# Sorted block attention with Fourier mixing on one core: the second half of V mixed in its own layout and turned through device memory

## The chip, the cores and the metric

The kernel runs on one core of a Trainium2 chip. The core has five engines with a queue of instructions each: TensorE (PE, with its weight loads PEld), VectorE (DVE), ScalarE (ACT), GpSimd (POOL) and SyncE (SP), the last two used here mostly to issue transfers. Data lies in on-chip memory with 128 partitions; PE writes its sums into eight PSUM banks of 128 partitions by 512 numbers, which DVE or ACT must empty. The metric is the time of one launch in microseconds on the device, smaller is better. The kernel before takes 257.36 us (median of three runs, 257.14 to 257.45).

## The reference

There are 4 batches, 8 heads, 768 positions and 64 channels per head, and the positions form 8 blocks of 96. A small 8×8 matrix per head, normalised five times over rows and columns, mixes the blocks of K and V; each block of Q attends to the one block at its place.

```python
for _ in range(5):
    P = P - np.max(P, axis=-1, keepdims=True)
    P = np.exp(P)
    P = P / (np.sum(P, axis=-1, keepdims=True) + 1e-09)
    P = P / (np.sum(P, axis=-2, keepdims=True) + 1e-09)
k_sorted = np.einsum('bhij,bhjcd->bhicd', P, k_b).reshape(B, H, S, D)
v_sorted = np.einsum('bhij,bhjcd->bhicd', P, v_b).reshape(B, H, S, D)
scores = scale * np.matmul(q_b, k_sb.transpose(0, 1, 2, 4, 3))
attn = softmax(scores);  x = heads_joined(np.matmul(attn, v_sb))
```

The heads are joined to x of 4 × 768 × 512, and the second part mixes it by a Fourier transform and sends it through a LayerNorm and a feed-forward network (FFN) of width 2048:

```python
u = x + np.real(np.fft.fft(np.fft.fft(x, axis=1), axis=2))
un = (u - mu) / np.sqrt(var + 1e-06)          # mean, variance over 512
out = u + np.maximum(un @ w_ch1, 0.0) @ w_ch2
```

## The kernel before

The matrices are normalised first, for all 32 pairs of batch and head. Then the four batches follow each other; the attention of later batches runs between the FFN products of earlier ones. For a batch, `kq_four` mixes K, `kqt` turns it (Q is turned by PE for the first batches and by transposing DMAs at L1188 afterwards), `scores` makes 96×96 score blocks, ACT takes exponentials (L1245), DVE or ACT subtracts one and writes f16 (L1258 or L1260), `av` multiplies by V (L1275) and DVE divides by the row sums (L1289, L1292). `dft1` and `dft2` are the Fourier mixing; `dft2` also adds x (L1453 for the first three tiles of a batch, L1467 and L1476 for the other three), makes the LayerNorm and has the result turned into the tile `ut`, by PE and a copy (L855) for batch 0 and by DMA (L1529) for the others. `ff1` is the first FFN product (L1558, emptied with a ReLU at L1570), `mlp` the second (L1615). Batches 2 and 3 use a form with seven products for eight, `ff1_seven` (L1694): ACT copies the running sum out of PSUM (L1714, tiles `vsf`), DVE adds it to another bank (L1702) and clamps the result at zero in place (L1708).

V is handled for two batches at a time: `t` = 0 is batches 0 and 1, `t` = 1 batches 2 and 3. It is loaded with one partition for each (batch, head, block) and, along the partition, 96 keys by 64 channels (`nat[t]`; `nat[1]` is a part of the tile `kq`, which K and Q of batch 3 use later). `v_path` finds each block's mean over keys, since the mean is treated apart, and rearranges V into `vcx` (eight instructions; for `t` = 1 each also subtracts the mean, L909). `v_mix(t, e)` multiplies 128-key columns of `vcx` with the block-diagonal matrices `bdv16[t]`, 64 small matmuls (L945) for a batch, which both mixes the blocks and brings the keys onto the partitions; eight evictions (L855) put the result into `vsb`, the V operand with 96 keys on the partitions and 64 channels and a one for each of 128 groups (a view of the tile `vsf`). Half `e` of `vsb` serves batch `e` and later batch 2 + `e`. The product `av` of any head waits for all eight evictions of its half. Later `vcx` holds sums of the FFN's hidden layer (`hs`, L1771).

The variance in the LayerNorm comes from two DVE instructions per tile (L1494, L1496). Only the first three tiles of batch 0 (`split`) do otherwise: the addition at L1453 leaves its row sum (an accumulator read follows it), a small DVE instruction divides it by 512, and ACT squares the tile around that mean and sums (L1488).

Nothing is issued in the order in which the code is written. `Plan` gives each operation a number, its costs and what it waits for, and the tables `ORDER` list, for each engine, the numbers in the order in which it issues them. Where the table leaves PE idle ahead of the first LayerNorm, by the costs in the plan, the code puts in matmuls that compute nothing (L1973, spin matmuls).

## Time and profile before

| | |
|---|---|
| median of 3 runs | 257.36 us (257.14 to 257.45) |
| span of the profiled execution | 254.8 us |
| instructions of the profiled execution | 7461 |
| PE busy | 245.2 us (96%) |
| DVE busy | 234.2 us (92%) |
| ACT busy | 165.3 us (65%) |
| PE clock over the span | full but for the last slice |
| moved by DMA | 26.54 MB, 104 GB/s on average |

The span runs from the first to the last instruction of the profiled execution. Its own time is the span of 254.8 us with what lies around it; the runs' median is 2.6 us above the span. Busy time is the sum over an engine's instructions as recorded; neighbouring ones can overlap a little. In a row such as `L909 DVE TENSOR_TENSOR vcx<-kq,vbn 128x768 f16<-128x768 f16 x8 | 11.6, 1473 | 0.0` stand the line of the code, the engine, the operation, the written and read tiles with their shapes, the count, the busy time in us, the mean in ns, and the idle time just before. Timeline and chain rows begin with the start and the duration in us. A row of DMA issues ends with the KB of one and the median time until it has landed.

### The profile page before, as it was taken

What the parts mean: (1) busy time and instruction counts of PE and PEld (TensorE: products, weight loads), DVE (VectorE), ACT (ScalarE), POOL (GpSimd) and SP (SyncE); (2) the same over time, 40 slices, a digit from 0 to 9 for tenths busy, and PEclk for the clock granted to TensorE, in tenths of its full rate; (3) what the DMA queues carried; (4) which work ended last, traced back from release to release, by engine and by line L of the source; (5) the groups of instructions that cost most, each with busy time, mean ns of one, the idle gap of its engine ahead of it and who ended that gap; (6) DMA issues with size and microseconds to landing.
All of it is one profiled execution on the core that took longest, in us unless ns stands there. A gap on an engine that the chain in (4) does not pass through costs nothing.

```text
span 254.8 us, 7461 instructions
## 1 busy us (share of the span) xinstructions
PE 245.2 (96%) x2996; PEld 167.0 (66%) x2996; DVE 234.2 (92%) x597; ACT 165.3 (65%) x376; POOL 57.5 (23%) x88
## 2 busy tenths in 40 slices
PE   4999999999999999999999999999999999999992
PEld 1347875566566676644667757888657887567882
DVE  4799998999999989978999998999999999999993
ACT  2599998999968879956797377622687323773000
POOL 8974532234400770003100000210100000050013
PEclk9999999999999999999999999999999999999998
DMA  6999999999942699524132002530202400220025
GB/s 134 202 215 300 210 217 214 208 211 187 150 49 75 86 193 120 64 43 136 44 38 44 1 8 46 98 125 35 82 3 41 84 3 0 85 88 37 3 82 207
DMA packets 42809, 26.54 MB, mean 104 GB/s; under 512 B 30234, under 2 KB 39208, under 8 KB 42772
## 3 DMA queue, kind: packets, MB, share of 16 engines
q0 software_dynamic: 23664, 18.35, 42.9%
q1 hardware_dynamic: 19110, 7.71, 15.0%
q8 instruction: 23, 0.38, 0.6%
q14 instruction: 12, 0.10, 0.1%
HBM read 29.07 MB, written 6.29 MB: 139 GB/s over the span
## 4 chain that ended last, share of the span: by engine, by line
PE 71%; issue 9%; DVE 9%; ACT 8%; POOL 2%; DMA 1%; POOLq 0%; DVEq 0%
PE bank L1558 15%; PE bank L1794 14%; PE bank L1694 12%; PE bank L1615 9%; PE bank L1275 4%; PE bank L1440 3%; PE bank L945 2%; PE bank L1236 2%; ACT vcx L855 2%; PE bank L1349 2%; POOL out_dram L1593 2%; DVE rt L1292 1%; PE bank L1444 1%; PE bank L1047 1%; PE bank L1140 1%
## 5 line engine op out<-in xcount | busy, mean ns | idle before, releaser
L1558 PE MATMUL bank<-ut,w1sb 128*128 128x384 f16 x256 | 48.2, 326 | 0.0
L1714 ACT COPY vsf<-bank 128x384 f32<-128x384 f32 x48 | 21.6, 482 | 24.0 <-PE bank L1694 23.6
L1245 ACT ACTIVATE ex<-bank 96x384 f32<-96x384 f32 x64 | 29.3, 487 | 7.6 <-PE bank L1236 6.2
L1558 PEld LDWEIGHTS <-w1sb 128*128 128x128 f16 x256 | 23.1, 98 | 14.1 <-issue 0.3
L1570 ACT ACTIVATE hr<-bank 128x384 f16<-128x384 f32 x56 | 26.3, 491 | 8.5 <-PE bank L1558 8.5
L1593 POOL DMA_INDIRECT out_dram<-u,rows x9 | 9.4, 1042 | 97.4 <-DVE u L1811 72.5
L1794 PEld LDWEIGHTS <-hr 128*128 128x128 f16 x288 | 28.2, 98 | 4.6
L1702 DVE TENSOR_TENSOR hr<-bank,vsf 128x384 f16<-128x384 f32 x48 | 25.2, 548 | 1.6 <-PE bank L1694 1.0
L1615 PE MATMUL bank<-w2sb,hr 128*128 128x512 f16 x96 | 23.6, 380 | 0.0
L1794 PEld LDWEIGHTS <-vcx 128*128 128x128 f16 x216 | 21.1, 98 | 3.2
L1694 PE MATMUL bank<-ut,w1sb 128*128 128x384 f16 x96 | 20.7, 326 | 0.0
L1794 PE MATMUL bank<-w2sb,hr 128*128 128x256 f16 x144 | 18.7, 272 | 0.0
L1275 PEld LDWEIGHTS <-eb 97*128 97x128 f16 x416 | 15.7, 98 | 3.1 <-issue 0.4
L1794 PE MATMUL bank<-kq,vcx 128*128 128x256 f16 x144 | 17.5, 272 | 0.0
L1694 PEld LDWEIGHTS <-w1sb 128*128 128x128 f16 x128 | 12.5, 98 | 7.5
L612 POOL DMA_DIRECT2D kq<-in_q_dram x18 | 15.4, 866 | 8.8 <-PE bank L1558 4.2
L1292 DVE TENSOR_TENSOR rt<-bank,rz 128x384 f16<-128x384 f32 x32 | 16.9, 547 | 0.2
L1275 PE MATMUL bank<-vsf,eb 97*128 97x65 f16 x416 | 16.9, 193 | 0.0
L855 ACT CAST ks<-bank 128x384 f16<-128x384 f32 x27 | 14.4, 555 | 3.1 <-PE bank L1140 3.0
L1260 ACT ACTIVATE eb<-ex,negone 96x384 f16<-96x384 f32 x26 | 15.9, 616 | 0.1
L855 ACT CAST vsf<-bank 96x512 f16<-96x512 f32 x22 | 14.2, 679 | 1.4 <-PE bank L945 1.4
L1258 DVE TENSOR_SCALAR eb<-ex 96x384 f16<-96x384 f32 x38 | 13.9, 371 | 0.6 <-ACT ex L1245 0.4
(195 smaller groups left out, 535.5 us busy)
## 6 DMA issues: line engine op xcount, KB each, us to landing
w1sb<-in_moe_w_ch_dram POOLq DMA_DIRECT2D x4, 512.0 KB, 18.6
w2sb<-in_moe_w_ch_dram POOLq DMA_DIRECT2D x4, 512.0 KB, 21.5
hr<-in_v_dram POOLq DMA_DIRECT2D x2, 768.0 KB, 8.8
kq<-in_v_dram POOLq DMA_DIRECT2D x2, 768.0 KB, 12.7
kq<-in_k_dram POOLq DMA_DIRECT2D x8, 192.0 KB, 6.5
kq<-in_q_dram POOLq DMA_DIRECT2D x16, 96.0 KB, 6.7
out_dram<-u SPq DMA_DIRECT2D x5, 256.0 KB
kq<-in_k_dram POOLq DMA_DIRECT2D x2, 384.0 KB, 11.7
```

The lines of the kernel that those rows point to most:

```text
L855: (nc.scalar.copy if e == "ACT" else V.tensor_copy)(dst, src)
L1245: nc.scalar.activation(ex.ap[0:96], pss[h2].ap[0:96, 0:384], AF.Exp, scale=SCALE),
L1260: nc.scalar.activation(ed, src, AF.Identity, bias=negone[0:96])
L1275: nc.tensor.matmul(po.ap[:, 65 * T:65 * T + 65], eb.ap[:, e0:e0 + 128], vsf[0:97, vi:vi + 65], start=(n == 0), stop=(n == len(WIN[T]) - 1) ...
L1292: P.add({"DVE": (0.465, 0.56)}, lambda _: V.tensor_tensor(rt.ap[:, :, D * h:D * h + D], po3()[:, :, 0:D], rz.ap[:, :, None].broadcast_to([ ...
L1558: nc.tensor.matmul(ps.ap[:, 0:GT], w1sb[:, c, 128 * fc:128 * fc + 128], ut.ap[:, c, :], start=(c == 0), stop=(c == 3))
L1570: nc.scalar.activation(hr[g][:, fc, :], ps.ap[:, 0:GT], AF.Relu)
L1615: nc.tensor.matmul(ps.ap, hr[g][:, fc, 128 * tt:128 * tt + 128], w2sb[:, fc, :], start=(fc == 0), stop=(fc == 15))
L1694: nc.tensor.matmul(ps.ap[:, 0:GT], lhs[:, c, fi], rhs()[:, c, :], start=(start and c == 0), stop=(c == 1), skip_group_check=True)
L1702: return P.add({"DVE": (0.47, 0.57)}, lambda _: V.tensor_tensor(hr[g][:, fc, :], p.ap[:, 0:GT], o.ap, op=ALU.add), r=r, w=hk(g, fc, fc + 1 ...
L1714: P.add({"ACT": act(GT)}, lambda _: nc.scalar.copy(x.ap, A.ap[:, 0:GT]), r=[A], w=[x], prio=pr_v - 1, tag="pc", after=avs)
L1794: nc.tensor.matmul(ps.ap[:, o:o + 256], lhs()[:, fc], rhs[:, fc], start=(start and fc == 0), stop=(fc == 7), skip_group_check=True)
```

## The change

For batches 2 and 3 the rearrangement of V on DVE and the two calls of `v_mix` go. In `v_turn` the block-diagonal matrices are the stationary operand instead: one matmul mixes the means, and 12 matmuls of 512 columns mix V as it lies in `nat[1]`, so that the blocks stay on the partitions. DVE subtracts the mixed mean on the way from PSUM to `vcx`, SP stores `vcx` in two halves (768 KB each) to a tensor `vmixed` in device memory, and `v_back` reads it in eight DMAs of 192 KB with the keys on the partitions, in pieces of 64 f16 numbers, into `vsb`. For batches 2 and 3 `av` waits only for the DMA that holds its own head, two heads to a DMA. What waited for the mixing matmuls (the sums in `vcx`) now waits for the two stores.

All 24 LayerNorm tiles use the `split` form, so that ACT has the squares of 21 more; for the last three tiles of a batch the row sum comes in two parts. In `ff1_seven` the addition and the clamp become one custom DVE instruction, max(min(a + b, largest float), 0). The priorities of the loads of the second FFN weights change slightly, and all tables of `ORDER` are new; in POOL's only the memory fills at the start move, while the spin matmuls go from 32 to 35.

```diff
+from concourse.dve_ops import TENSOR_ADD_SAT
...
 ORDER = {
     "PE": (
-        "77 69 78 73 79 91 139 123 125 127 92 97 129 211 141 143 0 103 218 "
...
+        "0 77 69 78 91 73 79 92 123 139 211 125 97 127 141 143 129 103 218 "
...
+FMAX = float(np.finfo(np.float32).max)
...
+    vdram = nc.dram_tensor("vmixed", [128, 96 * D], F16).ap()
...
     def v_path(t):
...
-        for n in range(8):
+        for n in range(0 if t else 8):
...
-                P.add({"DVE": dve(768, 1.0, 0.55)},
-                      lambda _, dst=dst, src=src, dr=dr: V.tensor_tensor(
-                          dst, src, vbn[:, dr, None, None].broadcast_to(
-                              [128, 16, 6, 8]), op=ALU.subtract),
-                      r=[("nat", 1, hf), "vbn"] + stage,
-                      w=[("vcx", n)], tag="vcd")
...
-    def v_mix(t, e):
+    def v_mix(e):
...
                       r=[(ps, 1) if n else ps, "pack"],
                       w=[(("bdv16", "bdv32")[n], t)],
                       tag="bdv32", prio=P.prio + 5 * t + 8 * n)
+
+    def v_turn():
+        n1 = nat[1]
+        stage = [i for n in range(4, 8) for i in kqk(n)]
+        bd = bdv16[1].rearrange("p g i -> p (g i)")
+        pm_ = Buf("pf")
+        mm_ = mean16.rearrange("p a m -> p (a m)").bitcast(F32)[:, 0:64]
+        P.add(pe(0.08, 1), lambda _: nc.tensor.matmul(
+            pm_.ap[:, 0:64], bd, vbn), r=["vbn", ("bdv16", 1)], w=[pm_],
+            tag="vmean")
+        P.add({"DVE": dve(64), "ACT": act(64)}, lambda e: copy(
+            e, mm_, pm_.ap[:, 0:64]), r=[pm_], w=["mean", "mhi", "mm1"],
+            tag="vmean")
+        for n in (0, 2, 4, 6, 8, 10, 1, 3, 5, 7, 9, 11):
+            ps = Buf("pm", "pf")
+            P.add(pe(mm(512), 1), lambda _, n=n, ps=ps: nc.tensor.matmul(
+                ps.ap.rearrange("p (c d) -> p c d", d=D), bd,
+                n1.rearrange("p (c r d) -> p r c d", r=6, d=D)[
+                    :, n // 2, 8 * (n % 2):8 * (n % 2) + 8, :]),
+                r=[("nat", 1, n % 2), ("bdv16", 1)] + stage, w=[ps],
+                tag="vmix")
+            P.add({"DVE": (0.6, 0.69)}, lambda _, n=n, ps=ps: V.tensor_tensor(
+                vcx[:, 512 * n:512 * n + 512].rearrange(
+                    "p (c d) -> p c d", d=D),
+                ps.ap.rearrange("p (c d) -> p c d", d=D),
+                mm_[:, None, :].broadcast_to([128, 8, D]), op=ALU.subtract),
+                r=[ps, "mm1"], w=[("vcx", i) for i in range(
+                    512 * n // 768, (512 * n + 511) // 768 + 1)], tag="vev")
+        for hf in range(2):
+            lo = 3072 * hf
+            vmixed.append(P.add(
+                {"SP": (0.6, 2.6)}, lambda _, lo=lo: nc.sync.dma_start(
+                    vdram[:, lo:lo + 3072], vcx[:, lo:lo + 3072]),
+                r=[("vcx", 4 * hf + i) for i in range(4)],
+                w=[("vdram", hf)], nbytes=786432, tag="vst"))
+
+    def v_back(e):
+        for n in range(4):
+            g = 64 * e + 16 * n
+            P.add({"SP": (0.6, 3.0)}, lambda _, g=g: nc.sync.dma_start(
+                vsb[0:96, g:g + 16, 0:D],
+                vdram[g:g + 16].rearrange("g (c d) -> c g d", d=D)),
+                r=[("vdram", 0), ("vdram", 1), "vsz"],
+                w=[("vsb", e, 2 * n + i) for i in range(2)], nbytes=VGB,
+                tag="vga")
 
     def a_path(t):
...
                         start=(n == 0), stop=(n == len(WIN[T]) - 1),
                         skip_group_check=True)
         av_ = P.add(pe(0.52, 13), f, r=[(eb, 0), (eb, 1), "erow", "vrow", "vsz"]
-              + [("vsb", b % 2, n) for n in range(8)], w=[po, (rts[b], "a", h)],
+              + [("vsb", b % 2, n) for n in (range(8) if b < 2 else [h])], w=[po, (rts[b], "a", h)],
               tag="av")
         if b == 3:
             avs.append(av_)
...
         mv = Buf("mv")
-        split = (b, g) == (0, 0)
+        split = True
...
                       r=[ps] + [(rt, h) for h in range(H)],
                       w=[u] + ([(mv, tt, 0)] if split else []), tag="u", prio=pv)
             else:
-                def f(_, u=u, ps=ps, T=T):
+                def f(_, u=u, ps=ps, T=T, tt=tt):
                     p_ = ps.ap
                     rev = bass.AP(
                         tensor=p_.tensor, offset=p_[:, 511:512].offset,
...
                         u.ap[:, 1:511].rearrange("p (m n) -> p m n", n=2),
                         rt.ap[:, T, 1:511].rearrange(
                             "p (m n) -> p m n", n=2),
-                        RSC, rev, op0=ALU.mult, op1=ALU.add)
+                        RSC, rev, op0=ALU.mult, op1=ALU.add,
+                        accum_out=mv.ap[:, tt, 0:1] if split else None)
                 P.add({"DVE": (0.6, 0.69)}, f,
-                      r=[ps] + [(rt, h) for h in range(H)], w=[u], tag="u", prio=pv)
-
-                def f(_, u=u, ps=ps, T=T):
+                      r=[ps] + [(rt, h) for h in range(H)],
+                      w=[u] + ([(mv, tt, 0)] if split else []), tag="u", prio=pv)
+
+                def f(_, u=u, ps=ps, T=T, tt=tt):
                     V.scalar_tensor_tensor(
                         u.ap[:, 0:512:511], rt.ap[:, T, 0:512:511], RSC,
-                        ps.ap[:, 0:512:256], op0=ALU.mult, op1=ALU.add)
+                        ps.ap[:, 0:512:256], op0=ALU.mult, op1=ALU.add,
+                        accum_out=mv.ap[:, tt, 1:2] if split else None)
                 P.add({"DVE": (0.1, 0.18)}, f,
-                      r=[ps] + [(rt, h) for h in range(H)], w=[u], tag="u", prio=pv)
+                      r=[ps] + [(rt, h) for h in range(H)],
+                      w=[u] + ([(mv, tt, 2)] if split else []), tag="u", prio=pv)
             if split:
                 sq = Buf("ex")
-                P.add({"DVE": (0.07, 0.15)}, lambda _, tt=tt: V.tensor_scalar(
-                    mv.ap[:, tt, 0:1], mv.ap[:, tt, 0:1], 1.0 / DM, None,
-                    op0=ALU.mult), r=[(mv, tt, 0)], w=[(mv, tt, 1)],
-                    tag="bna", prio=pv)
+
+                def f(_, tt=tt, T=T):
+                    a = mv.ap[:, tt, 0:1]
+                    if T < 3:
+                        V.tensor_scalar(a, a, 1.0 / DM, None, op0=ALU.mult)
+                    else:
+                        V.tensor_scalar(a, a, mv.ap[:, tt, 1:2], 1.0 / DM,
+                                        op0=ALU.add, op1=ALU.mult)
+                P.add({"DVE": (0.07, 0.15)}, f,
+                      r=[(mv, tt, 0)] + ([(mv, tt, 2)] if T > 2 else []),
+                      w=[(mv, tt, 1)], tag="bna", prio=pv)
                 P.add({"ACT": (0.72, 0.92)}, lambda _, tt=tt, u=u, sq=sq:
                       nc.scalar.activation(
                           sq.ap[:, 0:256].bitcast(F16), u.ap, AF.Square,
...
                              prio=pr_pe + 0.5 * i, tag="ff1", after=after)
 
             def add(g, fc, p, o, r):
-                return P.add({"DVE": (0.47, 0.57)}, lambda _: V.tensor_tensor(
-                    hr[g][:, fc, :], p.ap[:, 0:GT], o.ap,
-                    op=ALU.add), r=r, w=hk(g, fc, fc + 1), prio=pr_v,
-                    tag="fadd")
-
-            def relu(g, fc):
-                P.add({"DVE": (0.16, 0.24)}, lambda _: V.tensor_scalar(
-                    hr[g][:, fc, :], hr[g][:, fc, :], 0.0, None, op0=ALU.max),
-                    r=hk(g, fc, fc + 1), w=hk(g, fc, fc + 1), prio=pr_v,
-                    tag="relu")
+                return P.add({"DVE": (0.47, 0.57)}, lambda _: V._custom_dve(
+                    TENSOR_ADD_SAT, out=hr[g][:, fc, :], in0=p.ap[:, 0:GT],
+                    in1=o.ap, s0=FMAX, s1=0.0), r=r,
+                    w=hk(g, fc, fc + 1), prio=pr_v, tag="fadd")
+
             def snap():
                 x = Buf("vx")
                 P.add({"ACT": act(GT)}, lambda _: nc.scalar.copy(
...
             prod(D, X12, B21, w1k + ak, True, gate)
             x = snap()
             add(0, i, D, x, [D, x])
-            relu(0, i)
             prod(Q, G1, e_(E1), ["g1", E1], True)
             prod(A, G2, e_(E2), ["g2", E2], False)
             x2 = snap()
             ends.append(prod(A, G3, B12, w1k + [(ub, "d")], False))
             x = snap()
             add(1, i + 8, Q, x, [Q, x])
-            relu(1, i + 8)
             prod(A, X22, e_(E4), w1k + [E4], False)
             P.add({"ACT": act(GT)}, lambda _, A=A, i=i: nc.scalar.activation(
                 hr[0][:, i + 8, :], A.ap[:, 0:GT], AF.Relu), r=[A],
                 w=hk(0, i + 8, i + 9), prio=pr_v, tag="relu")
             prod(Q, G4, B22, ["g4"] + bk_, False)
             add(1, i, Q, x2, [Q, x2])
-            relu(1, i)
         for i in range(8):
             pair(i)
 
...
     at(-75.0, (v_path, (0,)))
     at(-60.0, (bdv_make, ()))
     at(-55.0, (v_mean, ()))
-    at(-50.0, (v_mix, (0, 0)))
+    at(-50.0, (v_mix, (0,)))
...
     for c in range(4):
-        load_w2(c, 62.0 + c, P.wr["nat", 1, 1])
+        load_w2(c, 61.0 + 0.1 * c, P.wr["nat", 1, 1])
     at(70.0, (v_path, (1,)))
-    at(12.0, (v_mix, (1, 0)), (v_mix, (1, 1)))
+    at(12.0, (v_turn, ()), (v_back, (0,)), (v_back, (1,)))
```

On ACT the second table load (`ACT_TABLE_LOAD`) now stands behind the first exponential of the matrices' normalisation instead of ahead of it. Besides, work moves between DVE and ACT: DVE does 49 of the 64 subtractions of one after an exponential (38 before), 22 of the ReLUs of `ff1` (8 before) and 14 of the 24 LayerNorm outputs (8 before).

The first place is DVE's queue between the Fourier additions of batch 0 (`eo`, `fq`) and its first sums `u`. The names are: `tkh` and `bdk` for the matrices that mix K, `ks` for mixed K, `qt` for turned Q, `eb` and `ex` for exponentials, `mv` for mean and variance. Before:

```order
L855 CAST tkh_109<-bank1_62 128x256
L1382 COPY vcx_74<-vcx_74 1x127
L832 TENSOR_TENSOR bdk_106<-tkh_109,perm_110 128x512
L855 CAST vsf_75<-bank7_68 96x64x8
L855 COPY qt0_79<-bank4_65 128x384
L1453 SCALAR_TENSOR_TENSOR u0_93,mv0_129<-rt0_85,bank0_61 128x512
L1483 TENSOR_SCALAR mv0_129<-mv0_129 128x1
L1453 SCALAR_TENSOR_TENSOR u1_94,mv0_129<-rt0_85,bank3_64 128x512
L1483 TENSOR_SCALAR mv0_129<-mv0_129 128x1
L1453 SCALAR_TENSOR_TENSOR u2_95,mv0_129<-rt0_85,bank4_65 128x512
```

After, with the lines of the changed file (L856 is the old L855, L1291 the old L1258, L1415 the old L1382, L1486 the old L1453; L881 is the reduction in `v_path`):

```order
L856 CAST ks1_78<-bank3_64 128x6x8x8
L856 COPY qt0_79<-bank2_63 128x384
L1291 TENSOR_SCALAR eb4_76<-ex0_82 96x4x96
L856 CAST ks1_78<-bank4_65 128x6x8x8
L1415 COPY vcx_74<-vcx_74 1x127
L1291 TENSOR_SCALAR eb4_76<-ex2_84 96x4x96
L856 CAST ks0_77<-bank2_63 128x6x8x8
L1291 TENSOR_SCALAR eb4_76<-ex1_83 96x4x96
L1291 TENSOR_SCALAR eb4_76<-ex0_82 96x4x96
L881 TENSOR_REDUCE vsum_115<-bank7_68 128x64
L1486 SCALAR_TENSOR_TENSOR u0_93,mv0_129<-rt0_85,bank3_64 128x512
L1291 TENSOR_SCALAR eb4_76<-ex2_84 96x4x96
```

Four of the subtractions (`eb4<-ex`), three casts of mixed K and the reduction for the mean of the second half of V (`vsum`) now stand ahead of the first `u` of batch 0, a fifth subtraction ahead of the second; the matrices for K (`tkh`, `bdk`) went farther ahead.

The second place is SP's queue around the transposes of Q for batch 2 (`qt<-kq`) and the stores of the output's first part (`out_0_dram`). Before:

```order
L1188 DMA_TRANSPOSE qt0_79<-kq_70 128x6x128
L1188 DMA_TRANSPOSE qt2_81<-kq_70 128x6x128
L1583 DMA out_0_dram<-u1_94 128x512
L1188 DMA_TRANSPOSE qt1_80<-kq_70 128x6x128
L1188 DMA_TRANSPOSE qt0_79<-kq_70 128x6x128
L1583 DMA out_0_dram<-u0_93 128x512
L1188 DMA_TRANSPOSE qt2_81<-kq_70 128x6x128
L1585 DMA out_0_dram<-u2_95 112x512
```

After:

```order
L1014 DMA vmixed<-vcx_74 128x3072
L1221 DMA_TRANSPOSE qt2_81<-kq_70 128x6x128
L1221 DMA_TRANSPOSE qt1_80<-kq_70 128x6x128
L1127 DMA rb_105<-rr_107 32x512
L1221 DMA_TRANSPOSE qt0_79<-kq_70 128x6x128
L1022 DMA vsf_75<-vmixed 96x16x64 x2
L1629 DMA out_0_dram<-u1_94 112x512
L1631 DMA out_0_dram<-u1_94 15x512
L1633 DMA out_0_dram<-u1_94 1x512
L1022 DMA vsf_75<-vmixed 96x16x64 x2
L1221 DMA_TRANSPOSE qt2_81<-kq_70 128x6x128
L1627 DMA out_0_dram<-u0_93 128x512
```

The second store of mixed V and the gathers (`vsf_75<-vmixed`) now stand between the transposes of Q and the stores of batch 0's `u`; the transposes of the next Q stand behind four of the gathers.

More of the change, by code (lines that the diff above doesn't have):

```diff
@@ L30 @@
 VBP = -1500.0
+VGB = 500000
 FETCH = (190, 255, 6.0, 3.5)
@@ L898, in v_path @@
             dst = vcd[:, dr, :, 8 * hf:8 * hf + 8]
[L899 to L913 removed]
+            c = {"ACT": act(768, 0.75)}
+            if n not in (0, 2):
+                c["DVE"] = dve(768)
+            P.add(c, lambda e, dst=dst, src=src: copy(e, dst, src),
+                  r=[("nat", 0, hf)] + half(hf),
+                  w=[("vcx", n)], tag="vcp",
+                  after=sks[30:31] if n in (0, 2) else sks[-1:])
     def v_mean():
```

46 lines of the change are left out of this document (16 added, 30 removed), and 199 rows, old and new, of the table ORDER.

## The prediction

> **What bounds the kernel now.** I read the page first, then busy time by stage, then the chain of waits, and last the timeline around the first FFN product.
>
> ```profile
> PE 245.2 (96%) x2996; PEld 167.0 (66%) x2996; DVE 234.2 (92%) x597; ACT 165.3 (65%) x376; POOL 57.5 (23%) x88
> ```
>
> Two engines are nearly full, so the averages do not choose between them. The next view gives, for two stretches of the span, the length and then the busy time of PE, PEld, DVE, ACT and POOL; the number behind POOL's is PE's clock.
>
> ```profile
> 13.56:28.76 15.20, 15.04 (x252) 10.21 (x251) 14.80 (x36) 14.48 (x32) 8.60 (x14) 1.00 1.23 248
> 28.76:49.44 20.68, 20.22 (x397) 13.22 (x392) 19.24 (x59) 19.25 (x47) 5.97 (x9) 1.00 1.10 214
> ```
>
> In them DVE has 14.80 of 15.20 us and 19.24 of 20.68 us. PE looks as full there, but its count contains the spin matmuls, which compute nothing: until the first LayerNorm PE is padded and DVE does the real work. The edges of the second stretch are the first softmax normalisation of batch 0 and the copy of its first transposed LayerNorm tile; behind that copy stands the first FFN product, and the last row is the last product of the program.
>
> ```profile
> 28.76 0.19 DVE L1289 RECIPROCAL rz<-bank 128x6 f32<-128x6 f32 x1
> 49.44 1.09 DVE L855 COPY ut<-bank 128x512 f16<-128x512 f16 x3 [0.28 <-PE bank L1537]
> 50.96 1.47 PE L1558 MATMUL bank<-ut,w1sb 128*128 128x384 f16 x8
> 249.23 1.04 PE L1794 MATMUL bank<-w2sb,vcx 128*128 128x256 f16 x8
> ```
>
> From 50.96 to 250.27 the chain runs on PE, in unbroken pieces late in the program:
>
> ```profile
> 184.98 10.40 PE bank L1694 x64
> ...
> 216.32 10.41 PE bank L1694 x64
> ```
>
> Ahead of those are short pieces of four products, some of 0.65 us and some of 0.76 us:
>
> ```profile
> 64.53 0.76 PE bank L1558 x4
> 66.74 0.65 PE bank L1558 x4
> 134.27 0.76 PE bank L1558 x4
> ```
>
> The 0.11 us more is a wait for a free bank, which DVE or ACT empties. The chain has some 14 of the longer kind, 1.5 us in all: that is all that a less loaded DVE can give back after 51 us. So the end is (when DVE lets the FFN begin) + (PE work then left), 50.96 + 199.31 = 250.27. The span of 254.8 us adds a tail of 4.5 us (last residual sum and stores), and the median of 257.36 lies 2.6 us above the span; neither is touched. All sums are made against the end at 250.27 and carried to the median.
>
> **The change, part by part.** *DVE instructions removed and added.*
>
> ```profile
> L909 DVE TENSOR_TENSOR vcx<-kq,vbn 128x768 f16<-128x768 f16 x8 | 11.6, 1473 | 0.0
> L1708 DVE TENSOR_SCALAR hr<-hr 128x384 f16<-128x384 f16 x48 | 10.3, 250 | 0.1
> L1494 DVE BATCH_NORM_STATS2 st<-u 128x6 f32<-128x512 f32 x15 | 10.2, 682 | 0.1
> L1496 DVE BATCH_NORM_AGGREGATE mv<-st 128x2 f32<-128x6 f32 x21 | 3.1, 167 | 0.0
> 44.32 0.08 DVE L1453 DVE_READ_ACCUMULATOR u<-rt,bank 128x1 f32 x1
> 44.44 0.15 DVE L1483 TENSOR_SCALAR mv<-mv 128x1 f32<-128x1 f32 x1
> 44.52 0.69 DVE L1453 SCALAR_TENSOR_TENSOR u<-rt,bank 128x512 f32<-128x512 f16 x1
> ```
>
> The last three rows follow each other at 0.12 and 0.08 us, so a DVE instruction starts about 0.08 us before the one ahead has ended by its record; I charge duration less 0.08. Out go 8 × 1.40 (V minus block mean), 48 × 0.17 (clamp), 21 × (0.60 + 0.09) (variance): 33.9 us. In come 12 evictions of 512 columns with a subtraction at about 0.60 (7.2), some 33 accumulator reads at 0.12 (4.0) and 21 small scalings at 0.07 (1.5). DVE loses about 21 us, nearly all behind 51 us, where PE alone sets the pace and 1.5 us at most comes of it. I take 0.3 us: the tables also move FFN evictions from ACT to DVE, which refills the room.
>
> *ACT.* It gains 21 squares of 0.72 + 0.19 us, 19 us in all, and hands work to DVE for it.
>
> ```profile
> L1488 ACT ACTIVATE ex<-u,mv 128x512 f16<-128x512 f32 x3 | 2.2, 722 | 0.0
> L1488 ACT ACTIVATION_READ_ACCUMULATOR ex<-u,mv 128x1 f32 x3 | 0.6, 186 | 0.0
> 0.74 1.28 ACT L711 ACT_TABLE_LOAD   x1 [0.74 <-PEq L1990]
> 4.58 0.26 ACT L766 ACTIVATE hr<-hr 32x64 f32<-32x64 f32 x1 [1.50 <-DVE hr L776]
> ```
>
> ACT is busy 65% of the span; in the second stretch it is as full as DVE (19.25), and relief there comes from DVE taking its work. The table load now stands between the first and second exponential, 1.28 us inside a wait of 1.50 us for DVE: nothing, at most 1.3 us if that cover is gone.
>
> *The start-up on DVE, which decides.* Up to the first normalisation DVE has 34 instructions for 36, about 13.5 us: with no idle time it ends at 13.56 + 13.5 = 27.1. From there to the first transposed tile DVE has 78 instructions where it had 54. Prices:
>
> ```profile
> L1258 DVE TENSOR_SCALAR eb<-ex 96x384 f16<-96x384 f32 x38 | 13.9, 371 | 0.6 <-ACT ex L1245 0.4
> L855 DVE CAST ks<-bank 128x384 f16<-128x384 f32 x5 | 2.9, 581 | 0.7 <-PE bank L1140 0.7
> L855 DVE CAST vsf<-bank 96x512 f16<-96x512 f32 x10 | 6.8, 684 | 0.2
> L1292 DVE TENSOR_TENSOR rt<-bank,rz 128x384 f16<-128x384 f32 x32 | 16.9, 547 | 0.2
> L1289 DVE RECIPROCAL rz<-bank 128x6 f32<-128x6 f32 x32 | 5.4, 181 | 1.1 <-PE bank L1275 0.9
> ```
>
> Ten more softmax subtractions (14 for 4) at 0.29 are 2.9; three K casts at 0.50 are 1.5; one Q^T copy 0.47; two of the new subtracting evictions 1.2; one more normalisation 0.10 + 0.47; the V mean's reduction 0.6, taken like a bank of 512; four accumulator reads 0.5; some six tiny ones 0.7; less one V cast, 0.6. Together 7.8 us: 18.6 us of work by the same count become 26.4. The two stretches had 3.1 us of DVE idle time by that count, at most as much is left, at least none; I take 2.0, nearer the old value, because its causes (PE, ACT) remain. The step from the copy to the first product was 1.52 us and gets 0.25 more for a second tile's part. So the FFN starts at 27.1 + 26.4 + 2.0 + 1.75 = 57.2.
>
> *PE work left behind that point.*
>
> ```profile
> 78.35 0.93 PE bank L945 x32
> 68.49 1.73 PE bank L1615 x8
> 137.37 1.60 PE bank L1275 x52
> 89.01 0.51 PE bank L1140 x48
> 99.55 0.46 PE bank L1236 x32
> ```
>
> The old mix of V is 128 matmuls, four times the first row, 3.7 us, all behind 51 us. The new one is 12 matmuls of 512 columns at 1.73 / 8 = 0.216: 2.6 us, of which 8 (1.7) come behind. Ahead of the first FFN product the tables now also put one attention head's two halves (52 matmuls, 1.6), one K mix (0.5), 16 scores and 24 transposes (about 0.6), and fewer switches of PE's shape (0.3). Left: 199.3 − 3.7 + 1.7 − 3.0 = about 194.3, say 194.2. Sum: 57.2 + 194.2 − 0.3 = 251.1, against 250.27: 0.8 us later.
>
> *The way through device memory.* SP's queue gets two stores of 768 KB and eight gathers of 192 KB, each of 1536 pieces of 128 bytes; the trace has no such gather.
>
> ```profile
> hr<-in_v_dram POOLq DMA_DIRECT2D x2, 768.0 KB, 8.8
> kq<-in_v_dram POOLq DMA_DIRECT2D x2, 768.0 KB, 12.7
> kq<-in_q_dram POOLq DMA_DIRECT2D x16, 96.0 KB, 6.7
> ut<-un SPq DMA_TRANSPOSE x18, 2.4
> SPq L1188 <- DMA kq<-in_q_dram: 24.1, 4, 11.0
> ```
>
> Between the last V product and the first attention product of batch 2 lie about 25 us of PE work. A store like the loads of its size takes 9 to 13 us, leaving 12 to 16 us for the first gathers; loads of 96 KB in 128-byte pieces land in 6.7 us, so a gather of twice that should take 7 to 13 us, several in flight at once. Each head waits only for its own gather, so the second, third and fourth pair of heads have 2.4, 18 and 22 us more. Cost taken: nothing. The other end is the four gathers of batch 2 one after the other, at twice 6.7 us each: 9 + 4 × 13.4 = 62.6 us for the fourth against 25 + 22, 16 us late. In series they are late from about 7 to 9 us each, by the second pair ((25 + 2.4 − 9 or 13) / 2). On SP the gathers stand behind the Q transposes of batch 2, which already waited up to 11.0 us for Q; and behind the gathers stand the output stores and, at the end of that row of them, the transposes of batches 2 and 3, so a late store would hold those too. The partial sums of the FFN's hidden layer, which overwrite `vcx`, now wait for the two stores where they waited for 128 matmuls; they come with batch 1's second FFN product, long after a store has landed.
>
> [...] I leave that outcome 1 in 100, inside the chance of the late gather below.
>
> *The clamp in one instruction.* The pair add (0.547) and clamp (0.250) becomes one instruction with the add's operands.
>
> ```profile
> L1702 DVE TENSOR_TENSOR hr<-bank,vsf 128x384 f16<-128x384 f32 x48 | 25.2, 548 | 1.6 <-PE bank L1694 1.0 <-ACT vsf L1714 0.3
> ```
>
> I take the add's price. PE needs 14 × 0.163 = 2.28 us for a pair of FFN tiles (10.40 us for 64), DVE three such adds, 1.4 us. Only above 0.76 us each would DVE set the pace.
>
> **The rivals.** *Start-up without idle time* (not slower). If DVE's 2.0 us of idle time vanish, because the variance no longer stands between two of its steps, and the bank waits go too (up to 1.5), the end is 250.3 + 0.8 − 0.7 to 3.0: 0.1 to −2.2 us, about 256.0. For it: 24 more instructions are there to fill gaps. Against it: the old gaps come from PE and ACT. It decides when idle time falls under 1.2 us. *Late gather* (slower): if store and first gather together exceed 25 us, PE waits for each pair at batch 2, +3 to +16 us, 260 to 273; the SP wait of 11.0 us speaks for it, the landing times against it. *Slow clamp* (slower): if the new instruction reads at half the speed, 0.87 us less overlap for 48 is 2.6 us a pair against 2.28, 16 pairs, +5.3 us, 262.7. Nothing in the trace shows it; an add with two full operands from PSUM and SBUF speaks against it.
>
> **How the numbers follow.** A change under 0.2% (0.5 us) could not be told from none. The forecast, +0.8 us, has 0.62, spread by the idle time (0 to 3.1) and the relief (0 to 1.5) over −1.4 to +2.2: some 0.13 of it is faster, 0.15 the same, 0.34 slower. Start-up without idle time has 0.22: 0.19 faster, 0.03 the same. Late gather has 0.10, slow clamp 0.06, all slower. Faster 0.32, same 0.18, slower 0.50. Time 257.36 + 0.8 = 258.2. The range reaches to 255.6 (−1.8) and to 261.0, the milder gather: outside lie the rest of the late gather, the slow clamp and the fastest end. The forecast's own range is 256.0 to 259.6.
>
> **What would show it.** Right: the first FFN product near 57 us, PE's chain unbroken from there, 194 us to the last product, DVE's total down by about 20 us with the span unchanged within 1%. Wrong: a first FFN product before 56 us (rival 1), PE idle in front of the first attention products of batch 2 with a DMA of the V tile as the releaser (late gather), or the new clamp's mean above 0.76 us (slow clamp). A stretch behind 57 us shorter than 193 us would mean that bank waits counted for more than I allow.

## The result, and the profile after

The changed kernel takes 269.64 us (median of four runs, 268.11 to 271.44) where the kernel before takes 257.25: 1.0482 times as long, with a 95% interval of 1.0452 to 1.0512. It is slower by 12.4 us; 0.8 us were forecast, and the range ended at 261.0.

The page of the changed kernel begins with each engine's busy time; its second part gives 40 slices of the span, of which PE's load and PE's clock are shown.

```profile
PE 248.5 (93%) x2884; PEld 166.4 (62%) x2884; DVE 226.6 (85%) x608; ACT 155.5 (58%) x361; POOL 57.7 (22%) x88
...
PE   4999999999996498999899999999999999999992
...
PEclk9999999999999599999999999999999999999998
```

DVE lost 7.6 us, not the 21 us that were counted (instructions removed less instructions added), because the tables moved other work to it; PE is idle and then slow in one place, around slices 13 and 14. The timeline of PE gives the places that matter: the first FFN product, the last product, and every wait of more than 1 us between them, with the product ahead of the long one.

```profile
57.60 1.46 PE L1602 MATMUL bank<-ut,w1sb 128*128 128x384 f16 x8
...
81.50 2.75 PE L1659 MATMUL bank<-w2sb,hr 128*128 128x512 f16 x12
90.27 0.85 PE L1269 MATMUL bank<-qt,ks 64*64 64x96 f16 x32 [6.01 <-DMA qt<-kq]
...
107.45 0.56 PE L1308 MATMUL bank<-vsf,eb 97*128 97x65 f16 x13 [1.29 <-DMA vsf<-vmixed]
...
260.11 1.91 PE L1830 MATMUL bank<-w2sb,vcx 128*128 128x256 f16 x16
```

The first FFN product starts at 57.60 us (57.2 forecast). The last product ends at 262.02, so 204.4 us follow it where 194.2 were forecast. PE waits 6.01 us for the turned Q of batch 2, and later 1.29 us for its V. The windows around the first wait (length, then busy time of PE, PEld, DVE, ACT, POOL, then PE's clock) show what comes on top:

```profile
80.00:84.00 4.00, 4.00 (x42) 2.09 (x38) 2.30 (x8) 0.00 (x0) 0.93 (x2) 1.00 1.38 197
84.00:88.00 4.00, 0.26 (x2) 0.00 (x0) 1.85 (x5) 0.00 (x0) 0.00 (x0) 0.93 1.88 119
88.00:92.00 4.00, 1.73 (x36) 1.11 (x37) 0.25 (x1) 1.15 (x3) 0.00 (x0) 0.50 1.98 134
92.00:96.00 4.00, 4.00 (x47) 1.81 (x46) 2.16 (x6) 1.96 (x5) 0.00 (x0) 0.72 1.46 149
```

During the wait PE's clock falls to 0.50, and it stays there until about 94.2 (0.72 on average over the last window leaves 2.24 us at half speed). Eight products of L1602 take 2.74 us there (from 91.06 us) and 1.47 us at the full clock (from 99.55 us). From 90.27 on that is 4.0 us of work at half speed, by estimate 2.0 us lost. The clock fell some 3.2 us into this wait of 6.01 us (0.93 on average over the second window), and some 2.2 us into a wait of 4.29 us in the run with Q first, below. Waits and clock together are 9.3 us of the 10.2 us that the stretch is too long; a wait of 0.8 us for a bank that DVE still reads is most of the rest.

Why Q came late stands in SP's queue, the start and the time each instruction held it (a row with x2 joins two neighbours, from the start of the first to the end of the second). First the kernel before, then the changed one:

```profile
65.03 3.42 SPq L1188 DMA_TRANSPOSE qt<-kq  x2
```

```profile
70.99 0.35 SPq L1014 DMA_DIRECT2D vmixed<-vcx  x1
...
74.81 0.53 SPq L1014 DMA_DIRECT2D vmixed<-vcx  x1
75.52 6.66 SPq L1221 DMA_TRANSPOSE qt<-kq  x2
82.23 0.83 SPq L1127 DMA_DIRECT2D rb<-rr  x1
83.22 2.29 SPq L1221 DMA_TRANSPOSE qt<-kq  x1
85.67 4.94 SPq L1022 DMA_DIRECT2D vsf<-vmixed  x2
```

The transposes of batch 2's Q, which were issued from 65.03 us in the kernel before, now stand behind the two stores. The first store waits until 70.99 for DVE's subtractions; the second leaves at 74.81, behind DVE's last subtraction (it ends at 72.76) and three small transfers for the Fourier part. The transposes start 10.5 us later and then hold the queue for 2.9 to 3.6 us each where the first two in the kernel before held it for 1.3 to 1.9 (3.42 us together). Q then reaches PE only at 90.27, some 8 us after the second transpose has left the queue; what slows the transposes there is not separated by the runs below.

### The profile page after: what moved, and what is told of

Same layout as the page of the kernel before. It is cut to its first block, busy times and chain, and to the rows that moved or that the text cites. A ratio compares the mean times of both kernels' runs of the same rounds, so it can differ in the third digit from the quotient of the medians.

```text
span 267.3 us, 7218 instructions
## 1 busy us (share of the span) xinstructions
PE 248.5 (93%) x2884; PEld 166.4 (62%) x2884; DVE 226.6 (85%) x608; ACT 155.5 (58%) x361; POOL 57.7 (22%) x88
## 4 chain that ended last, share of the span: by engine, by line
PE 58%; issue 20%; DVE 10%; DMA 6%; POOL 3%; ACT 2%; POOLq 0%; DVEq 0%
PE bank L1830 17%; PE bank L1738 14%; PE bank L1602 11%; DMA kq<-in_q_dram 4%; PE bank L1308 2%; DMA out_dram<-u,rows 2%; PE bank L1473 2%; PE bank L1382 2%; POOL out_dram L1637 2%; DVE eb L1291 1%; PE bank L1269 1%; PE bank L874 1%; POOL kq L613 1%; PE bank L2009 1%; PE bank L998 1%
## 5 line engine op out<-in xcount | busy, mean ns | idle before, releaser
L1602 PE MATMUL bank<-ut,w1sb 128*128 128x384 f16 x256 | 49.3, 332 | 0.0
L1602 PEld LDWEIGHTS <-w1sb 128*128 128x128 f16 x256 | 24.1, 99 | 17.3 <-issue 2.1
L1746 DVE CUSTOM_DVE_ANT_0 hr<-bank,vsf 128x384 f16<-128x384 f32 x48 | 24.9, 553 | 4.7 <-PE bank L1738 3.9
L1291 DVE TENSOR_SCALAR eb<-ex 96x384 f16<-96x384 f32 x49 | 17.6, 375 | 8.1 <-ACT ex L1278 7.9
L1614 ACT ACTIVATE hr<-bank 128x384 f16<-128x384 f32 x42 | 19.5, 486 | 4.4 <-PE bank L1602 4.1
L1738 PE MATMUL bank<-ut,w1sb 128*128 128x384 f16 x96 | 21.0, 326 | 0.0
L613 POOL DMA_DIRECT2D kq<-in_q_dram x18 | 15.0, 840 | 12.4 <-DMA kq<-in_q_dram 3.8
L1269 PE MATMUL bank<-qt,ks 64*64 64x96 f16 (+1 forms) x448 | 10.7, 215 | 6.8 <-DMA qt<-kq 6.0
L1738 PEld LDWEIGHTS <-w1sb 128*128 128x128 f16 x128 | 12.5, 98 | 6.9
L1637 POOL DMA_INDIRECT out_dram<-eb,rows x3 | 2.9, 977 | 60.0 <-ACT vsf L1753 45.8
L1269 PEld LDWEIGHTS <-ks 64*64 64x64 f16 (+1 forms) x448 | 7.6, 111 | 13.1 <-DMA qt<-kq 6.5
```

The lines of the kernel that those rows point to most:

```text
L1269: nc.tensor.matmul(pss[h2].ap[c, BLK * j:BLK * j + BLK], ks.ap[rows, 4 * g + j, c], qt.ap[rows, c0:c0 + BLK])
L1291: V.tensor_scalar(ed, src, -1.0, None, op0=ALU.add)
L1602: nc.tensor.matmul(ps.ap[:, 0:GT], w1sb[:, c, 128 * fc:128 * fc + 128], ut.ap[:, c, :], start=(c == 0), stop=(c == 3))
L1614: nc.scalar.activation(hr[g][:, fc, :], ps.ap[:, 0:GT], AF.Relu)
L1637: st_ = [nc.gpsimd.indirect_dma_start(out.rearrange("b s m -> (b s) m"), bass.IndirectOffsetOnAxis(ap=rows[:, i:i + 1], axis=0), u.ap, None)]
L1738: nc.tensor.matmul(ps.ap[:, 0:GT], lhs[:, c, fi], rhs()[:, c, :], start=(start and c == 0), stop=(c == 1), skip_group_check=True)
```

## The experiments

Three edits of SP's and POOL's order first. `q_first` puts two transposes of Q ahead of the first store and one ahead of the second (a table of numbers; in it 582, 596 and 610 are the transposes, 462 and 463 the stores, 420 to 423 rows for the Fourier part):

```diff
-  "... 232 462 421 423 422 463 582 596 420 610 470 468 ..."
+  "... 232 582 596 462 421 423 422 610 463 420 470 468 ..."
```

> On SP alone, the first two transposes of Q for batch 2 go ahead of the first store of mixed V and the third ahead of the second store; nothing else changes. Theory 1 (queue): the 6.0 us for which PE waits at the first scores of batch 2 come from these transposes standing behind the stores, which wait for DVE until 74.8 us. Then the wait goes, and with it the stretch of 6.8 us at half clock: about 259 to 261 us. Theory 2 (crowding): the transposes are slow because batch 3's loads of K and Q, now 15 us earlier, share the DMA engines with them. Then they land hardly earlier and the time stays at 267 to 270 us.

`b3_late` lets batch 3's loads of K and Q wait for the first scores of batch 2 (`sc2` collects these):

```diff
         after = lns[1:2] if b > 1 else ()
+        if b == 3:
+            after = sc2[0:1]
...
```

> Batch 3's loads of K and Q wait for the first scores of batch 2, as late as they came in the kernel before; SP's order is that of the changed kernel. Theory 1 (queue): the transposes are still issued at 75.5 us behind the second store, so that most of the wait stays: 265 to 269 us. Theory 2 (crowding): without the loads beside them the transposes land in time, the wait goes: 259 to 261 us.

> Both edits together. Both theories: no wait at batch 2's scores and full clock, leaving the start-up that the prediction costed and 194 us of PE work: 258 to 260 us. If it stays above 262 us, a third cause is at work, the gathers or the custom instruction.

Measured: 267.22 us, 1.0398 (1.0373 to 1.0423) with Q first; 270.52 us, 1.0512 (1.0475 to 1.0549) with batch 3 late; 267.55 us, 1.0409 (1.0391 to 1.0426) with both. For both together either theory had 258 to 260 us, so a third cause is at work. Crowding by batch 3's loads falls as a cause: PE waits as long for Q without them (this row is of the run with batch 3 late).

```profile
90.62 0.86 PE L1271 MATMUL bank<-qt,ks 64*64 64x96 f16 x32 [5.74 <-DMA qt<-kq]
```

The queue as the cause is only half right. With Q first the first transpose is issued at 64.64 us, the second is through at 74.55 (one row below), and the wait for Q is gone. But PE now waits for V, some 9 us behind where Q had come late, and the half clock follows there:

```profile
64.64 9.91 SPq L1221 DMA_TRANSPOSE qt<-kq  x2
...
81.14 0.61 SPq L1014 DMA_DIRECT2D vmixed<-vcx  x1
...
89.32 1.10 SPq L1022 DMA_DIRECT2D vsf<-vmixed  x2
...
92.73 1.30 SPq L1022 DMA_DIRECT2D vsf<-vmixed  x2
```

```profile
99.46 0.90 PE L1308 MATMUL bank<-vsf,eb 97*128 97x65 f16 x13 [4.29 <-DMA vsf<-vmixed]
```

So of the loss only 2.4 us came back, and another wait had stood behind the first one.

`spin_fill` was to keep the clock up during the wait:

```diff
             def f(_, g=g, pss=pss):
+                if (b, hp, g) == (2, 0, 0):
+                    for _ in range(26):
+                        nc.tensor.matmul(pss[0].ap[:, 0:480], idh,
+                                         pack[:, 0:240].bitcast(F16))
                 for j in range(4):
```

> The changed kernel with 26 matmuls of 480 columns that compute nothing (0.2 us each, 5.2 us) ahead of the first scores of batch 2, so that PE is busy while it waits for Q. If the half clock (0.50 from 87.3 to 94.1 us) comes from the idle PE, the clock stays at 1.0 and the time falls by the 3 to 4 us of which PE's work there is stretched, half of it 1.9 us: about 267.5 us, the wait for the transposes unchanged. If the clock falls for another reason, the time stays at 269 to 270 us or grows.

It missed its aim: 275.06 us, 1.0700 (1.0683 to 1.0718). Other scores of batch 2 come first in PE's order, so the 26 matmuls ran behind the wait (the row with L1265).

```profile
91.46 0.53 PE L1274 MATMUL bank<-qt,ks 64*64 64x96 f16 x16 [6.92 <-DMA qt<-kq]
91.92 7.37 PE L1265 MATMUL bank<-pack 128*128 128x480 f16 x26
```

So no edit kept the clock up through a wait; only removing the wait did (in the run with Q first and the gathers in order of use, below, the clock is 1.00 in every window from 80 to 104 us). The run tells little of the pace either: it is 5.4 us slower, but the useless matmuls took 7.4 us instead of 5.2, since 11 of the 26 ran at half clock (4.34 us for these), the wait ahead of them was 0.9 us longer, and less of PE's other work fell into the slow stretch. Work added to PE here was not hidden; that is all.

Next the way through device memory was taken out. `no_trip` leaves out stores and gathers, `no_gather` the gathers alone; batches 2 and 3 then use the V of batches 0 and 1.

```diff
-                {"SP": (0.6, 2.6)}, lambda _, lo=lo: nc.sync.dma_start(
-                    vdram[:, lo:lo + 3072], vcx[:, lo:lo + 3072]),
+                {"SP": (0.6, 2.6)}, lambda _, lo=lo: None,
...
-            P.add({"SP": (0.6, 3.0)}, lambda _, g=g: nc.sync.dma_start(
-                vsb[0:96, g:g + 16, 0:D],
-                vdram[g:g + 16].rearrange("g (c d) -> c g d", d=D)),
+            P.add({"SP": (0.6, 3.0)}, lambda _, g=g: None,
```

> The changed kernel with neither the two stores nor the eight gathers: batches 2 and 3 use the V that batches 0 and 1 left in the tile, so that their output is not the reference's. Everything else, the matmuls and subtractions of the new mixing too, is as in the changed kernel. If the way through device memory is the whole loss against the forecast, PE waits neither for Q nor for V, the clock stays full, the first FFN product stays at 57.6 to 58.1 us and 194 us follow: 258 to 259.5 us. If the custom instruction or the squares on ScalarE cost as well, it stays above 260.5 us.

> The changed kernel without the eight gathers, the two stores kept (the output is not the reference's). Theory 1 (Q's transposes wait behind the stores, on SP and in its ring): the wait of about 6 us at the first scores of batch 2 stays, with the half clock behind it, and only the 1.5 us wait for V goes: 267 to 269 us. Theory 2 (the gathers crowd the transposes out): the wait at the scores shrinks below 2 us: 259 to 262 us.

Without the trip: 260.11 us, 1.0119 (1.0097 to 1.0140). Without the gathers alone: 268.39 us, 1.0447 (1.0421 to 1.0473). The trip is 9.5 us of the 12.4 us, and the rest of the change 2.9 us. The two stores suffice for the wait for Q, the gathers are not needed for it (run without the gathers):

```profile
90.03 0.85 PE L1267 MATMUL bank<-qt,ks 64*64 64x96 f16 x32 [5.89 <-DMA qt<-kq]
```

`store_pool` issues the stores from POOL's queue, between the loads of batches 2 and 3.

```diff
-                {"SP": (0.6, 2.6)}, lambda _, lo=lo: nc.sync.dma_start(
+                {"POOL": (0.8, 2.6)}, lambda _, lo=lo: nc.gpsimd.dma_start(
```

> The two stores are issued from POOL's queue, between batch 2's and batch 3's loads, instead of SP's; the output is the reference's. Theory 1 (queue): the first transposes are issued near 65 us as in the kernel before and PE does not wait at the scores of batch 2; the stores leave when DVE is done (71 and 75 us), so the gathers come before 95 us, where PE first wants them: 258 to 260 us. Theory 3 (the round trip itself is too long for its slack of 25 us, whatever the queue): the scores do not wait, but the first attention product of batch 2 waits 3 to 5 us for V, as in the run with Q first: 264 to 268 us.

269.65 us, 1.0476 (1.0452 to 1.0500). Again no wait for Q, and the wait for V has become the longer one; the rows are POOL's stores, SP's first four gathers with the output store between them, and the product that waits.

```profile
71.79 0.56 POOL L1015 DMA_DIRECT2D vmixed<-vcx  x1 [6.54 <-DVE eb L1292]
73.58 0.55 POOL L1015 DMA_DIRECT2D vmixed<-vcx  x1 [1.23 <-ACT un L1563]
```

```profile
80.83 4.25 SPq L1023 DMA_DIRECT2D vsf<-vmixed  x2
85.19 5.22 SPq L1630 DMA_DIRECT2D out_dram<-u  x1
...
91.24 3.19 SPq L1023 DMA_DIRECT2D vsf<-vmixed  x2
```

```profile
100.54 0.90 PE L1309 MATMUL bank<-vsf,eb 97*128 97x65 f16 x13 [6.00 <-DMA vsf<-vmixed]
```

Here the gathers begin at 80.83 and V is still not there at 94.5, though a load of Q, half their size, landed in 6.7 us in the kernel before (the median of 16). Which gather stands where would explain it: in the changed kernel's table the eight come in the order batch 3 heads 4 and 5, batch 3 heads 0 and 1, batch 2 heads 6 and 7, batch 2 heads 0 and 1, and so on. The one that PE wants first is the fourth, in the pair from 91.24. That is a theory that can be tried alone, in SP's table (464 to 467 are batch 2's gathers in order of heads, 468 to 471 batch 3's):

```diff
-  "... 470 468 947 467 464 624 935 466 941 465 471 675 525 469 ..."
+  "... 464 465 947 466 467 624 935 468 941 469 470 675 525 471 ..."
```

It was run with Q first, with the stores on POOL, and by itself.

> The run with Q's transposes first, and the eight gathers in the order in which their heads are used: heads 0 and 1 of batch 2 first, batch 3's last. In the changed kernel the gather that the first attention products of batch 2 wait for is the fourth in SP's queue, behind two for batch 3 and one for batch 2's last heads. Theory 4 (order of the gathers): the way through device memory would have fitted its slack, but the wanted piece comes fourth; the wait of 4.3 us for V goes, the clock stays full, and the time falls to that without the way through memory, 260 to 261 us. Theory 3 (the round trip is too long in any order): most of the wait for V stays, 264 to 267 us.

> The run with the stores in POOL's queue, and the gathers in the order of use. Theory 4: the wait of 6 us for V before batch 2 and that of 1.3 us behind it go, 260 to 261 us, about as with Q first. Theory 3: the wait for V stays above 3 us, 264 to 268 us.

> The changed kernel with only the eight gathers put in the order of use; the transposes of Q stay behind the stores. If the two orders cost separately, PE still waits about 6 us for Q at the scores of batch 2, with the half clock behind it, and only the 1.5 us wait for V goes: 267 to 268.5 us. If the early gathers for batch 3 are what slows the transposes, the wait for Q shrinks too: below 264 us.

With Q first: 260.29 us, 1.0127 (1.0108 to 1.0147). With the stores on POOL: 261.12 us, 1.0163 (1.0138 to 1.0188). Alone: 269.17 us, 1.0451 (1.0405 to 1.0498). The wait that is left in the last run is that for Q (6.50 us; that for V is gone), and the first attention product of batch 2 in the first waits for nothing although its gather is issued only at 88.80:

```profile
90.97 0.85 PE L1269 MATMUL bank<-qt,ks 64*64 64x96 f16 x32 [6.50 <-DMA qt<-kq]
```

```profile
88.80 1.10 SPq L1022 DMA_DIRECT2D vsf<-vmixed  x2
...
92.20 1.40 SPq L1022 DMA_DIRECT2D vsf<-vmixed  x2
```

```profile
94.86 0.56 PE L1308 MATMUL bank<-vsf,eb 97*128 97x65 f16 x13
```

The four cases side by side:

| | gathers as in the changed kernel | gathers in order of use |
|---|---|---|
| Q behind the stores | 269.64 us | 269.17 us |
| Q ahead of the stores | 267.22 us | 260.29 us |

Alone the edits bring 2.4 and 0.5 us (the 0.5 lie within the scatter of the runs, 267.98 to 270.36 against 268.11 to 271.44), together 9.4 us, nearly all that leaving the trip out brings (260.11 us). Two waits lay one behind the other, and the first hid most of the second.

The clamp in one instruction was tried by itself, in the kernel before (its 48 additions take the custom instruction, its 48 clamps go):

```diff
-  lambda _: V.tensor_tensor(hr[g][:, fc, :], p.ap[:, 0:GT], o.ap, op=ALU.add)
+  lambda _: V._custom_dve(TENSOR_ADD_SAT, out=hr[g][:, fc, :],
+                          in0=p.ap[:, 0:GT], in1=o.ap, s0=FMAX, s1=0.0)
```

> The kernel before with the addition and the clamp in one custom instruction and the 48 separate clamps gone; nothing else. Forecast's reading (PE bounds that stage, DVE has 1.9 us of work for 2.28 us of PE per pair of tiles): no change, 257.0 to 257.4 us. If the custom instruction were slower than the addition by half or more, or DVE bounded the stage, it would show: +2 us or more, or -1 us or more.

257.44 us, 1.0013 (1.0003 to 1.0022). The rows are DVE's group and the page's first line:

```profile
L1704 DVE CUSTOM_DVE_ANT_0 hr<-bank,vsf 128x384 f16<-128x384 f32 x48 | 24.7, 552 | 6.6 <-PE bank L1696 5.1 <-ACT vsf L1715 1.2
```

```profile
PE 245.3 (96%) x2996; PEld 167.1 (65%) x2996; DVE 226.7 (89%) x549; ACT 165.4 (65%) x376; POOL 58.5 (23%) x88
```

The custom instruction costs what the addition did (552 ns against 548), DVE is 7.5 us less busy, and the kernel is no faster: at these instructions DVE now waits 6.6 us, mostly for PE, where it waited 1.6 us at the additions before.

Whether DVE sets the start-up was tried in the kernel without the trip, by doing five subtractions ahead of the first LayerNorm twice:

```diff
                     if e == "DVE":
                         V.tensor_scalar(ed, src, -1.0, None, op0=ALU.add)
+                        if b == 1 and hp < 2:
+                            V.tensor_scalar(ed, src, -1.0, None, op0=ALU.add)
```

> The run without stores and gathers, with the subtractions behind the exponentials done twice on DVE in the first two pairs of heads of batch 1; five of them lie ahead of the first LayerNorm's transposed tile (0.29 us each, 1.45 us). If DVE alone sets when the first FFN product begins, as forecast, that product moves from 57.6 to about 59.0 us and the time from 260.1 to about 261.5 us. If PE or ACT set it, the product moves by less than 0.5 us.

262.01 us, 1.0193 (1.0165 to 1.0222), 1.9 us above the run without the trip, where the first FFN product starts at 57.60 too. Here it starts 2.2 us later. That is more than the 1.45 us expected, but at 375 ns each, their mean in the changed kernel, the five doubled subtractions are by estimate 1.9 us:

```profile
59.84 1.46 PE L1601 MATMUL bank<-ut,w1sb 128*128 128x384 f16 x8
```

Last, the variances were taken back to DVE in the best of the runs that compute the reference's output (`own` stands for the first three tiles of batch 0; the row sums in the additions go as well):

```diff
                 def f(_, tt=tt, T=T, u=u):
                     a = mv.ap[:, tt, 0:1]
-                    if T < 3:
+                    if not own:
+                        st = P.pools["st"][tt][2]
+                        V.bn_stats(st, u.ap)
+                        V.bn_aggr(mv.ap[:, tt, :], st)
+                    elif T < 3:
...
-                      nc.scalar.activation(
+                      own and nc.scalar.activation(
```

> The first kernel of this set with the variances taken back from ScalarE: for the 21 tiles DVE has the two statistics instructions again (0.69 us more each, less the small scaling and the accumulator reads, some 9 us in all), ACT has no squares. Forecast's reading: nearly all of it lies behind the first FFN product where PE sets the pace, so the time is that of the first kernel of this set within 1 us. If the variances on ScalarE are worth more, it is slower by 2 us or more; if the squares cost by keeping ACT from banks and exponentials, it is faster by 1 us or more.

271.97 us, 1.0581 (1.0559 to 1.0603), 11.7 us above the same kernel with the variances on ScalarE. Its page, behind that of the run it was made from:

```profile
PE 245.4 (95%) x2884; PEld 165.3 (64%) x2884; DVE 226.3 (87%) x608; ACT 155.5 (60%) x361; POOL 57.8 (22%) x88
```

```profile
PE 249.9 (93%) x2884; PEld 165.6 (61%) x2884; DVE 238.4 (88%) x596; ACT 141.7 (52%) x319; POOL 57.6 (21%) x88
```

DVE has 12.1 us more, and the kernel is longer by nearly as much, though PE should have set the pace. Between the first and the last FFN product PE now waits 8.1 us for DVE, in 13 places, where it waited 1.3 us in one; the rest is not in waits that the trace names. In the new order DVE has taken over other work. Whether the cost comes from the load or from the place, in the chain from the sum to the FFN, was not separated.

No version beat the kernel before; the nearest is Q first with the gathers in order of use, 3.4 us slower in the comparison of its own runs.

## Why the prediction was wrong, and where it was right

- **What bounds the kernel: right for the start-up, too simple behind it.** DVE sets the start-up: an estimated 1.9 us of doubled work moved the first FFN product by 2.2 us and the time by 1.9 us. Behind it PE is nearly full in the run without the trip (idle for 1.0 of 195.3 us), but DVE is not free there, as "PE alone sets the pace" had it: 12.1 us more on DVE cost 11.7 us. DVE's total, forecast about 20 us lower, fell by 7.6 us.
- **Start-up on DVE: right in sum.** 57.2 us forecast for the first FFN product, 57.60 measured. The parts err in opposite ways: the first normalisation came at 28.18 us instead of 27.1, the first transposed tile was copied at 56.33 us, not at 55.5, and the product followed after 1.27 us instead of 1.75.
- **PE work left: right within about 1 us.** 204.4 us less the waits of 6.0, 1.3 and 0.8 us and the 2.0 us of half clock is 194.3; 194.2 was forecast. In the run without the trip, with no such wait taken off, it is 195.3 us. The 0.3 us for fewer switches of PE's shape had no row beside it and was the author's estimate.
- **The way through device memory: this step failed.** The prediction put "Cost taken: nothing" beside stores, gathers and the transposes. It looked at the slack of the first gather against V and said that "the gathers stand behind the Q transposes of batch 2"; that the stores stand ahead of those transposes, and themselves wait for DVE, stood in the quoted order of SP's queue and was not costed. It also took the first gather in the queue for the first one needed, which is the fourth. The slack itself was sized well (from the last V product at 68.6 us to the first attention product of batch 2 at 94.86 in the run with both repairs, 26 us against 25), but the second store left only at 74.81, 6 us into it. The runs put 9.5 us on the step: a wait for Q, with a wait for V right behind, and the half clock.
- **The rival of the late gather** had a chance of 0.10, and the measured time lies in its 260 to 273 us, but in part by luck. Its place was half right: with Q first, or the stores on POOL, PE waits 4.3 to 6.0 us for V, but in the changed kernel the long wait is for Q, and only 1.29 us are for V.
- **The bank waits** were to give back 0.3 us. That the 0.11 us in the longer pieces is such a wait is not shown: the two quoted (from 64.53 and 134.27 us) follow products of L1236 on 64 × 64, the shorter one (from 66.74 us) follows products of L1275 on 97 × 128. In the runs without a wait for the trip there are small waits instead, 1.3 us at one place in the run with both repairs:

```profile
122.75 0.36 PE L1269 MATMUL bank<-qt,ks 64*64 64x96 f16 x16 [1.29 <-DVE u L1511]
```

  The span of the run without the trip is 258.1 us, and the forecast's sum was 255.6 (251.1 and the end of 4.5). Of the difference 0.4 us are start-up, 1.4 us the stretch of PE work (195.3 us against 194.2 less 0.3), and 0.7 us the end behind the last product, which is 5.2 us long instead of 4.5.
- **The clamp and the table load: right.** 553 ns against 547 as costed, and no gain in time. The table load's 1.28 us lie between two exponentials, and 0.20 us of waiting for DVE is still left behind it.
- **The outcome given 1 in 100**, gathers far slower than the loads, came from no row or run of this case, and no run shows it: in the run with both repairs the gather that the first product needs is issued from 88.80 us on and is there by 94.86, when that product runs without a wait, so under 6.1 us for 192 KB.

## What to carry to other kernels

When a change puts transfers into a queue, list what stands behind each of them there, and for which instruction of the pacing engine it is needed; here two stores, the first of which waited for DVE until 70.99 us, stood ahead of the first transpose, which went at 75.52 us and, ahead of the stores, at 64.64. Check also that the transfers are issued in the order in which they are used: a slack counted for the first of them is worth nothing if the one needed stands fourth (4.29 us of waiting for V with Q first, none in order of use). And when one repair brings little, look for the next wait behind the first before giving up its theory: here two repairs brought 2.4 and 0.5 us alone and 9.4 us together.

## What the runs showed of the hardware

- In six runs PE waited 4.29 to 6.92 us for Q or V, and by its means over windows of 4 us the clock fell to 0.50 some 2.2 to 5.1 us into the wait: 3.2 us into 6.01 (changed kernel), 2.2 into 4.29 (Q first), 5.1 into 6.50 (order of use alone), 2.6 into 6.00 (stores on POOL), 4.1 into 5.89 (no gathers), 4.5 into 6.92 (added matmuls). It stayed there for 6.8 to 6.9 us, with Q first for at least 6.6 us, up to the end of the windows, into the work that followed; in the changed kernel this was by estimate 2 us of the loss. In two more runs, with waits of 5.74 us (batch 3 late) and 3.99 us (both), a fortieth of the span stands at 0.5. The wait of 1.29 us in the changed kernel left the clock at 1.00 from 104 to 112 us.
- A gather of 192 KB in pieces of 128 bytes, keys onto partitions, landed within 6.1 us when it was the first of the gathers (issued from 88.80 us on, in use at 94.86 us, in the run with Q first and the gathers in order of use). Two transposes of Q held SP's queue for 3.42 us together in the kernel before and for 6.66 us in the changed kernel, behind a store of 768 KB; that the store is the reason is not shown, for with Q first the third transpose, also behind a store, held it for only 1.36 us.
- The custom instruction that adds and clamps took 552 ns for 128 × 384 in the kernel before and 553 ns in the changed kernel, the plain addition 548 ns.
